# A fused attention and MoE kernel on one core: the first tokens' part with features on partitions, order-only edges behind it, 1 MB weight pieces

## The chip, the cores and the metric

One Trainium2 chip, of which the kernel uses one core. The metric is the device time of one execution in microseconds (us). The engines are named as in the profile: PE (TensorE matmul) and PEld (its weight loads), DVE (VectorE), ACT (ScalarE), POOL (GpSimd), SP (SyncE, which here issues every DMA).

## The reference

Attention with a local causal softmax and a linear memory, gated per head, then a squared-ReLU MLP over the tokens (B=4, H=8, S=576, D=64; 2304 tokens, d_model 512, d_ff 2048):

```python
scores = 1/sqrt(D) * q @ k.T                     # causal, softmax over keys
local = softmax(scores) @ v
q_p = where(q > 0, q, exp(q) - 1) + 1
mem_out = (q_p @ M_prev) / (q_p . z_prev + 1e-6)
g = sigmoid(beta)
x = g * mem_out + (1 - g) * local                # (B*S, 512)
out = relu(x @ w_in)**2 @ w_out
```

The weights come as 64-bit floats, so the kernel has to make numbers that TensorE takes from pairs of 32-bit words.

## The kernel before

Every matrix product of the MLP runs in three terms, high by high, high by low, low by high. `split_weight` makes the high and the low part of each weight piece (128 rows of 512 numbers, 32 pieces, 512 KB each): DVE shifts the low word (line 163), ACT scales the high word (164), DVE merges both (165), ACT copies the high part (168), DVE subtracts (169). Each piece comes by one DMA on SP's queue (line 193); pieces 0 to 11 are the first stage, 12 to 22 the second, 23 to 31 the third and fourth, and a later stage's raw buffers take the place of earlier ones.

The tokens are worked in blocks of 256. Block 0 is the first 64 tokens of each of the four sequences; their attention and memory part is `first_tokens` (two groups of two sequences). The MLP of block 0 (`moe(0)`) needs the result of `first_tokens` as `xh` and `xl`, then the weight pieces as they come. The other tokens' attention runs in units of one sequence, one pair of heads and two or four query tiles (`attention`), beside the MLP of earlier blocks. The last two blocks are done together by `moe_pair`, 512 columns at a time.

`first_tokens` before the change holds the query rows on partitions for the memory part: exp on ACT (272), two DVE operations to make phi (273, 274), a product with `z` and a sum over the features on DVE (275, 276), the norm (277 to 279) and a scaling (280). The softmax is: mask (285), maximum (288), subtract (289), exp over all 512 columns (290), sum (291), norm (292 to 294), scaling (295). `outputs` then transposes both halves with eight 128x128 matmuls per group (304), copies them by ACT (306), and multiplies with `v` and `M` in sixteen matmuls per group (315).

A scheduler sets the order of each engine's queue; `first_tokens` has high priority in it. The generators are merged as

```python
merge((attn(0, 1), 12), (wsteps(13), 12))
merge((attn(1, FIRST), 52), (wsteps(33), 20), (first(), 18))
```

so the first attention units, the weights and the first MLP block interleave. SP's transfers take eight semaphores in turn: each is issued only when the one eight places ahead of it has landed.

Of the kernel before, what the change touches and what calls it, by code (L numbers as in the profile page):

```python
# [12 lines left out]
U32 = mybir.dt.uint32  # L13
AF = mybir.ActivationFunctionType
# [7 lines left out]
P = 128  # L22
# [9 lines left out]
PAIR = 0  # L32
# [10 lines left out]
PXT = 'up'  # L43
# [12 lines left out]
SEQ = 'a0 b0 g a1 b1 c0 c1 r l r r r r'  # L56
# [9 lines left out]
TE = ['dd', 'dd', 'dd', 'dd', 'dd']  # L66
TC = 'aa'
TW = 2 * NP * 6 * D
GB = 2
GN = GB * NP  # L70
GD = GN * D
TAGS = [0, 16, 16, 16, 18]


FIRST = 4
AFTER = mybir.DependencyInfo(mybir.DependencyClass.NoSync, mybir.DependencyReason.DATA)
# [14 lines left out]
def fused_kernel(ctx: ExitStack, tc: tile.TileContext, t0_d, zt_d, kk_d, qv_d, beta, w_in, w_out, out):  # L91
# [14 lines left out]
    nc.vector.tensor_copy(identb, idt)  # L106
    mask = cp.tile([P, MW], BF16, name="mask")
# [13 lines left out]
    gpb = cp.tile([P, GN], F32, name="gpb")  # L121
    g1b = cp.tile([P, GN], F32, name="g1b")

    def gates():
        nc.scalar.activation(gpm, gpm, AF.Exp, scale=-1.0)
        nc.vector.tensor_scalar(out=gpm, in0=gpm, scalar1=1.0, scalar2=None, op0=ALU.add)
        nc.vector.reciprocal(gpm, gpm)
# [4 lines left out]

        for b in range(GB):
            nc.vector.tensor_copy(gpb[:, b * NP : (b + 1) * NP], gp)
        nc.vector.tensor_scalar(out=g1b, in0=gpb, scalar1=-1.0, scalar2=1.0, op0=ALU.mult, op1=ALU.add)
# [3 lines left out]
    nc.vector.tensor_copy(mask0[D:], mask[D:, 512 : 512 + D])  # L139

# [16 lines left out]
    def split_weight(n):  # L157
        for rw, c0, c1 in raw.pop(n):
# [4 lines left out]
            nc.vector.tensor_scalar(out=u0, in0=u0, scalar1=29, scalar2=None, op0=ALU.logical_shift_right)  # L163
            nc.scalar.activation(f1, f1, AF.Prelu, scale=2.0**-111, alpha=-(2.0**32))  # L164
# [60 lines left out]
    def first_tokens(tp, ahead):  # L225
        me, ze, se, xe, ye = ([nc.gpsimd if c == "p" else nc.vector for c in t] for t in TE)
# [5 lines left out]
        tr, sp, wt0, wx = ({} for _ in range(4))  # L232
# [3 lines left out]
        for step in SEQ.split():  # L236
            if step == "r":
                ahead()
            elif step == "l":
                nxt.append(loads(*order[0]))  # L240
            elif step == "g":
                load_beta()
            else:
                g = int(step[1])
                if step[0] == "a":
                    nc.sync.dma_start(tr[g][:, : 2 * GD], t0_d[g, :, : 2 * GD])
                elif step[0] == "b":
                    nc.sync.dma_start(tr[g][:, 2 * GD : 3 * GD], t0_d[g, :, 2 * GD : 3 * GD])
                    for h in range(2):
                        nc.sync.dma_start(  # L250
                            tr[g][h * D : (h + 1) * D, 3 * GD : 4 * GD], zt_d[2 * g + h].partition_broadcast(D)
                        )
                else:
                    nc.sync.dma_start(tr[g][:, 4 * GD :], t0_d[g, :, 3 * GD :])

        def part(g, o, n):
            return tr[g][:, GD * o : GD * (o + n)].rearrange("p (i x) -> p i x", i=GN)

        def scores(g):
            sp[g] = sp0[:, g]  # L260
            qd = tr[g][:, : 2 * GD].rearrange("p (r i d) -> p i r d", r=2, i=GN)
            for i in range(GN):
                for h in range(2):
                    hd = slice(h * D, (h + 1) * D)
                    nc.tensor.matmul(sp[g][hd, i], qd[hd, i, 0], qd[hd, i, 1], start=True, stop=True)

        def phi(g):
            qn, zb = part(g, 2, 1), part(g, 3, 1)
            wt0[g] = tp.tile([P, GN, P], F32, tag="w", name="w", bufs=2)
            f = wt0[g][:, :, D:]  # L270
            t2 = tp.tile([P, GN], F32, tag="t2", name="t2", bufs=2)
            nc.scalar.activation(f, qn, AF.Exp)
# [606 lines left out]
```

## Time and profile before

| what | us |
|---|---|
| three runs | 584.8, 581.32, 584.38 (median 584.38) |
| the profiled execution, its time | 583.52 |
| its span, first to last instruction | 581.7 |
| PE busy in the span | 544.9 |
| DVE busy | 406.3 |
| ACT busy | 349.3 |

Busy times are unions over an engine's instructions; neighbouring instructions of one engine overlap a little, so the distance from start to start is shorter than an instruction's own time. The execution's own time is 1.8 us more than its span. DMA moved 75.72 MB in all.

### The profile page before, as it was taken

The numbers are of one execution on the slowest core, as the hardware profiler recorded it, in microseconds if no ns is written. First come the engines' busy times: TensorE is split into PE (matmuls) and PEld (weight loads), VectorE is DVE, ScalarE is ACT, GpSimd is POOL, SyncE is SP. The second block draws the span as 40 slices with busy tenths as digits, with TensorE's granted clock in tenths as the row PEclk, the third lists the DMA queues.
The fourth block names the chain that finished last, engine by engine and source line by source line (L and its number), as shares of the span: only waits on it lengthen the run. The fifth ranks groups of instructions, "written<-read, shape, count | busy, mean of one in ns | idle before, by whom it ended". The sixth has DMA issues, their size and how long they took to land.

```text
span 581.7 us, 11097 instructions
## 1 busy us (share of the span) xinstructions
PE 544.9 (94%) x4019; PEld 469.7 (81%) x4019; DVE 406.3 (70%) x1338; ACT 349.3 (60%) x794; POOL 39.4 (7%) x36
## 2 busy tenths in 40 slices
PE   2179999999999999999999999999999999999996
PEld 2058888787889788888888889888889898888885
DVE  5999989979968788998796888869887422000000
ACT  2779897667867667797567665566756222222222
POOL 1100011010100000000000000000000000222221
PEclk9998999999999999999999999999999999999999
DMA  8959386666375458885554636585235400000001
GB/s 283 372 176 368 94 254 194 155 143 158 96 153 135 117 134 189 148 200 155 128 136 95 148 99 155 111 178 139 55 90 114 110 16 1 36 1 0 1 0 73
DMA packets 125462, 75.72 MB, mean 130 GB/s; under 512 B 97248, under 2 KB 110560, under 8 KB 125408
## 3 DMA queue, kind: packets, MB, share of 16 engines
q1 hardware_dynamic: 125408, 75.02, 48.8%
q8 instruction: 31, 0.51, 0.4%
q14 instruction: 23, 0.19, 0.1%
HBM read 42.63 MB, written 8.78 MB: 88 GB/s over the span
## 4 chain that ended last, share of the span: by engine, by line
PE 62%; DVE 22%; DMA 9%; ACT 4%; issue 2%; SPq 1%; ACTq 0%; DVEq 0%
PE oacc L713 6%; PE oacc L711 6%; PE oacc L712 6%; PE up L723 6%; PE up L722 6%; PE up L721 6%; PE sp L467 4%; DVE e L486 3%; PE up L672 2%; PE up L671 2%; PE up L670 2%; DVE a L546 2%; DMA aT<-a 2%; DVE w L169 2%; PE pm L435 2%
## 5 line engine op out<-in xcount | busy, mean ns | idle before, releaser
L721 PE MATMUL up<-xh,w 128*128 128x256 f32 x448 | 129.0, 288 | 0.9 <-ACT xh L319 0.7
L723 PE MATMUL up<-xh,w 128*128 128x256 f32 x448 | 129.3, 289 | 0.0
L722 PE MATMUL up<-xl,w 128*128 128x256 f32 x448 | 128.3, 286 | 0.3 <-DVE xl L320 0.3
L506 ACT ACTIVATE e<-e,mx 128x320 f32<-128x320 f32 (+3 forms) x128 | 77.7, 610 | 54.9 <-DVE memx L586 35.4
L721 PEld LDWEIGHTS up<-xh,w 128*128 128x128 f32 x448 | 86.3, 193 | 5.0 <-ACT xh L319 1.0
L711 PE MATMUL oacc<-w,gh 128*128 128x512 f32 x224 | 90.2, 403 | 0.0
L712 PE MATMUL oacc<-w,gh 128*128 128x512 f32 x224 | 88.9, 397 | 0.0
L722 PEld LDWEIGHTS up<-xl,w 128*128 128x128 f32 x448 | 86.2, 192 | 3.0 <-issue 0.6
L723 PEld LDWEIGHTS up<-xh,w 128*128 128x128 f32 x448 | 86.2, 192 | 1.3 <-issue 0.7
L713 PE MATMUL oacc<-w,gl 128*128 128x512 f32 x224 | 85.4, 398 | 0.8 <-DVE gl L733 0.8
L546 DVE SCALAR_TENSOR_TENSOR a<-e,a 128x128 f16<-128x128 f32 x116 | 66.0, 577 | 24.1 <-ACT a L544 23.6
L678 DVE CAST gh<-r 128x512 fp32r<-128x512 f32 x16 | 6.8, 428 | 78.6 <-ACT r L677 78.6
L544 ACT ACTIVATE a<-e 128x128 f16<-128x128 f32 x116 | 55.1, 525 | 9.5 <-DMA aT<-a 9.1
L727 ACT ACTIVATE r<-up 128x512 f32<-128x512 f32 x56 | 32.9, 588 | 42.6 <-PE up L723 25.2
L713 PEld LDWEIGHTS oacc<-w,gl 128*128 128x128 f32 x224 | 40.9, 188 | 9.3 <-DVE gl L733 1.9
L711 PEld LDWEIGHTS oacc<-w,gh 128*128 128x128 f32 x224 | 42.2, 188 | 7.5 <-ACT hw L164 0.8
L712 PEld LDWEIGHTS oacc<-w,gh 128*128 128x128 f32 x224 | 42.3, 189 | 6.6
L486 DVE CUSTOM_DVE_ANT_0 e<-sp,mask 128x320 f32<-128x320 f32 (+3 forms) x128 | 47.2, 415 | 0.0
L676 ACT ACTIVATE r<-up 128x512 f32<-128x512 f32 x16 | 9.6, 599 | 62.1 <-PE up L672 62.1
L679 POOL TENSOR_TENSOR gl<-r,gh 128x512 fp32r<-128x512 f32 x16 | 20.7, 1292 | 379.9 <-DVE gh L678 379.9
L733 DVE TENSOR_TENSOR gl<-r,gh 128x512 fp32r<-128x512 f32 x56 | 39.1, 699 | 2.9 <-ACT gh L730 1.7
L576 PE MATMUL acc<-vs,aT 128*128 128x128 f16 x302 | 36.5, 220 | 0.0
(153 smaller groups left out, 1131.1 us busy)
## 6 DMA issues: line engine op xcount, KB each, us to landing
raw<-in_w_in_dram SPq DMA_DIRECT2D x11, 512.0 KB, 8.3
vv<-in_qv_dram SPq DMA_DIRECT2D x16, 320.0 KB, 3.1
raw<-in_w_out_dram SPq DMA_DIRECT2D x9, 512.0 KB, 8.1
kd<-in_kk_dram SPq DMA_DIRECT2D x16, 288.0 KB, 3.2
out_dram<-o SPq DMA_DIRECT2D x16, 256.0 KB, 2.1
xd<-memx SPq DMA_DIRECT2D x31, 128.0 KB, 2.1
xn<-xd SPq DMA_DIRECT2D x14, 256.0 KB, 2.7
qm<-in_qv_dram SPq DMA_DIRECT2D x8, 321.0 KB, 3.1
```

The costliest lines, as they stand in the source:

```text
L486: nc.vector.tensor_tensor_reduce(out=e[:, h, ka:kb], in0=sps[:, h, cs], in1=mask[:, 448 - q0 + ka : 448 - q0 + kb], scale=-0.125, scalar=3 ...
L506: ex = nc.scalar.activation(e[:n, h, :ke], e[:n, h, :ke], AF.Exp, bias=bs, scale=-1.0, accum_out=sm[:n, h : h + 1])
L544: nc.scalar.mul(av[:, :, o0 : o0 + w], x, SC)
L546: nc.vector.scalar_tensor_tensor(out=av[:, :, o0 + w : o0 + 2 * w], in0=x, scalar=SC, in1=av[:, :, o0 : o0 + w], op0=ALU.mult, op1=ALU.sub ...
L576: nc.tensor.matmul(o2, aT[:, h * nb + c, :n], vs[:, h, c], start=False, stop=c == i)
L711: nc.tensor.matmul(acc[t], gh[:, u, ts], w_out_op(f, 0), start=f == 0, stop=False)
L712: nc.tensor.matmul(acc[t], gh[:, u, ts], w_out_op(f, 1), start=False, stop=False)
L713: nc.tensor.matmul(acc[t], gl[:, u, ts], w_out_op(f, 0), start=False, stop=f == NF - 1)
L721: nc.tensor.matmul(up[:, u, :], w_in_op(f, k, 0), xh[:, k, :], start=k == 0, stop=False)
L722: nc.tensor.matmul(up[:, u, :], w_in_op(f, k, 0), xl[:, k, :], start=False, stop=False)
L723: nc.tensor.matmul(up[:, u, :], w_in_op(f, k, 1), xh[:, k, :], start=False, stop=k == NK - 1)
L733: (nc.vector if n in GLV else nc.gpsimd).tensor_tensor(out=gl, in0=r, in1=gh.bitcast(F32), op=ALU.subtract)
```

## The change

- The first tokens' input comes as one array with features on partitions: `a` (q, k and z of a group, 128x1032) and `c` (M and v, 128x1024). The separate array of broadcast `z` rows is gone.
- The memory norm is made by TensorE: sixteen matmuls with one column (`nr`), a DVE operation and a reciprocal on 128x8, and sixteen matmuls that spread the result over the features (`rb`); DVE then scales phi by it. The softmax's subtraction and sum go into ACT's exp, which is issued eight times per group on 64 columns with a bias and an accumulator. Only the softmax is transposed (`px0`, sixteen 64x64 matmuls), and M and v are applied in 32 matmuls per group.
- Weight pieces in pairs (`PAIR = 1`): two pieces are one DMA of 1 MB and one instruction of 1024 columns per step, nine pairs in all. For pieces 0 to 7 the shift moves from DVE to ACT (an Identity over the top 16 bits).
- `later` adds edges that set order only: the weight shift of pieces from 8 and ACT's scaling of them, and the first attention unit's exp and matmuls, are queued behind the first tokens' operations of the same engine.
- The sequence of the first transfers changes (`SEQ`).
- `moe_pair`: the low part of the squared hidden values is made by DVE instead of POOL, the accumulators lie in other PSUM buffers, and the last matmuls are ordered so that one token tile after another ends and is written out.

```diff
-PAIR = 0
+PAIR = 1
-SEQ = 'a0 b0 g a1 b1 c0 c1 r l r r r r'
+SEQ = 'a0 g a1 r r c0 l r r c1'
+WE = 8
...
+    def later(eng, x):
+        if eng in gate:
+            tc.add_manual_dep(x.ins, gate[eng].ins.name, AFTER, reason="first tokens lead")
+        return x
...
-            nc.vector.tensor_scalar(out=u0, in0=u0, scalar1=29, scalar2=None, op0=ALU.logical_shift_right)
-            nc.scalar.activation(f1, f1, AF.Prelu, scale=2.0**-111, alpha=-(2.0**32))
+            if n < 8:
+                top = rw.bitcast(U16).rearrange("p n (t h) -> p n t h", h=2)[:, :, 0, 1]
+                nc.scalar.activation(u0, top, AF.Identity, scale=2.0**-13, bias=half[:, :1])
+            else:
+                later("v", nc.vector.tensor_scalar(out=u0, in0=u0, scalar1=29, scalar2=None, op0=ALU.logical_shift_right))
+            prelu = nc.scalar.activation(f1, f1, AF.Prelu, scale=2.0**-111, alpha=-(2.0**32))
+            if n >= WE:
+                later("s", prelu)
...
-            ze[g].tensor_tensor(out=zb, in0=zb, in1=f, op=ALU.mult)
-            nc.vector.reduce_sum(out=t2, in_=zb, axis=AX.X)
+            for i, hd in pairs():
+                nc.tensor.matmul(nr[hd, i : i + 1], f[hd, i], z[hd, i : i + 1], start=True, stop=True)
+            nc.vector.scalar_tensor_tensor(out=t2, in0=nr, scalar=1e-6, in1=gib, op0=ALU.add, op1=ALU.mult)
             nc.vector.reciprocal(t2, t2)
-            se[g].tensor_tensor(out=f, in0=f, in1=t2[:, :, None].to_broadcast(bc), op=ALU.mult)
+            for i, hd in pairs():
+                nc.tensor.matmul(
+                    rb[hd, i], t2[hd, i : i + 1].to_broadcast([D, D]), ident[hd, hd], start=True, stop=True
+                )
+            nc.vector.tensor_tensor(out=f, in0=f, in1=rb, op=ALU.mult)
...
-            xe[g].tensor_tensor(out=e, in0=e, in1=t1[:, :, None].to_broadcast(bc), op=ALU.subtract)
-            nc.scalar.activation(e, e, AF.Exp)
-            nc.vector.reduce_sum(out=t1, in_=e, axis=AX.X)
+            for i in range(GN):
+                nc.scalar.activation(
+                    e[:, i], e[:, i], AF.Exp, bias=t1[:, i : i + 1], scale=-1.0, accum_out=ts[:, i : i + 1]
+                )
...
-                for i in range(NP):
-                    nc.tensor.transpose(px[:, i], wt0[g][:, b * NP + i], ident)
+            for i, hd in pairs():
+                nc.tensor.matmul(px[hd, i], et[g][hd, i], ident[hd, hd], start=True, stop=True)
+            gate["s"] = nc.scalar.copy(ex, px)
...
+            for i, hd in pairs():
+                nc.tensor.matmul(xp[hd, i], m[hd, i], ft[g][hd, i], start=True, stop=False)
+                gate["t"] = nc.tensor.matmul(xp[hd, i], v[hd, i], ex[hd, i], start=False, stop=True)
...
-            nc.gpsimd.tensor_tensor(out=gl, in0=r, in1=gh.bitcast(F32), op=ALU.subtract)
+            nc.vector.tensor_tensor(out=gl, in0=r, in1=gh.bitcast(F32), op=ALU.subtract)
...
+        for x, tokens in ((three, (0, 1)), (two, (0, 1)), (one, (0, 1)), (two, (2,)), (one, (2,)), (two, (3,)), (one, (3,))):
+            mms = down(*x, tokens=tokens)
+            if x is one:
+                for t in tokens:
+                    evict(t)
```

How the queues stand. ACT's queue, first before, then after, from the exp of the second group's queries; `raw` are the weight words, `w` with a number a weight's high or low part, `w` alone the first tokens' softmax values, `t` its row maxima, and `e` the first attention unit's scores.

```order
L272 ACTIVATE w<-tr_119 128x8x64
L164 ACTIVATE raw_141<-raw_141 128x512
L380 ACTIVATE pe<-qm 128x256
L290 ACTIVATE w<-w 128x8x64 x2
L164 ACTIVATE raw_149<-raw_149 128x512
L168 CAST w_98<-raw_141 128x512
L164 ACTIVATE raw_151<-raw_151 128x512
L164 ACTIVATE raw_153<-raw_153 128x512
L506 ACTIVATE e,sm<-e,mx 128x320
```

```order
L282 ACTIVATE f<-tr_117 128x512
L178 ACTIVATE raw_133<-raw_133,half 128x1024
L181 ACTIVATE raw_133<-raw_133 128x1024
L178 ACTIVATE raw_135<-raw_135,half 128x1024
L181 ACTIVATE raw_135<-raw_135 128x1024
L187 CAST w_100<-raw_133 128x1024
L306 ACTIVATE w,ts<-w,t_267 128x64 x8
L306 ACTIVATE w,ts<-w,t_337 128x64 x3
L187 CAST w_101<-raw_135 128x1024
L306 ACTIVATE w,ts<-w,t_337 128x64 x4
L178 ACTIVATE raw_144<-raw_144,half 128x1024
L181 ACTIVATE raw_144<-raw_144 128x1024
```

Before, one weight piece stood ahead of the softmax's two exps; now two pairs stand ahead of sixteen, and two passes of the third pair ahead of the last one. The attention unit's exps are not in this stretch any more.

DVE's queue around the first tokens' softmax, first before, then after; `sp` are its scores, and `nr` is the new norm in PSUM.

```order
L285 SCALAR_TENSOR_TENSOR w<-sp_157,mask_86 128x8x64
L280 TENSOR_TENSOR w<-w,t_175 128x8x64
L288 TENSOR_REDUCE t_212<-w 128x8
L276 TENSOR_REDUCE t_202<-tr_119 128x8
L288 TENSOR_REDUCE t_254<-w 128x8
L163 TENSOR_SCALAR raw_141<-raw_141 128x512
L289 TENSOR_TENSOR w<-w,t_212 128x8x64
```

```order
L136 TENSOR_SCALAR gs<-gpm 128x8
L184 SCALAR_TENSOR_TENSOR raw_133<-raw_133 128x1024
L288 SCALAR_TENSOR_TENSOR t_167<-nr,gib 128x8
L300 SCALAR_TENSOR_TENSOR w<-sp_149,mask_88 128x512 x2
L289 RECIPROCAL t_167<-t_167 128x8
L303 TENSOR_REDUCE t_267<-w 128x8
L303 TENSOR_REDUCE t_337<-w 128x8
L184 SCALAR_TENSOR_TENSOR raw_135<-raw_135 128x1024
```

The merge of the first weight pair now stands ahead of the mask, and the sums and subtractions are gone.

PE's queue where the first MLP block begins, first before, then after; `up` is the MLP's first product, `acc` and `pxa` belong to the first attention unit, `pm` and `sp` to its memory part and scores.

```order
L521 MATMUL pxa<-identr,e 64x128
L521 MATMUL pxa<-identr,e 128x128
L721 MATMUL up<-xh,w_98 128x256
L565 MATMUL acc<-vv,aF 128x64 x6
L722 MATMUL up<-xl,w_98 128x256
L723 MATMUL up<-xh,w_98 128x256
```

```order
L323 MATMUL xp<-wx,tr_117 64x64
L481 MATMUL sp<-kd,qm 128x320 x2
L481 MATMUL sp<-kd,qm 128x192 x2
L447 MATMUL pm<-qm,pe 128x130 x2
L749 MATMUL up<-xh,w_100 128x256 x2
L750 MATMUL up<-xl,w_100 128x256
L751 MATMUL up<-xh,w_100 128x256
L749 MATMUL up<-xh,w_100 128x256
```

The last two of ten transposes `pxa` and six `acc` matmuls of the first attention unit are seen ahead of the MLP's products before; they and a second group of scores, further ahead, stand behind the MLP's first products now.

## Rows read from the trace of the kernel before

**Rows 1.** The page's first part: busy us, share of the span, instructions.

```profile
PE 544.9 (94%) x4019; PEld 469.7 (81%) x4019; DVE 406.3 (70%) x1338; ACT 349.3 (60%) x794; POOL 39.4 (7%) x36
```

**Rows 2.** Windows: length, busy us (instructions) of PE, PEld, DVE, ACT, POOL; clock, DMA share, GB/s.

```profile
0.00:5.00 5.00, 0.56 (x10) 0.56 (x12) 1.00 (x3) 1.58 (x2) 1.82 (x8) 1.00 0.64 198
5.00:10.00 5.00, 1.67 (x32) 1.48 (x30) 3.07 (x13) 0.84 (x2) 0.00 (x0) 1.00 0.99 283
10.00:15.00 5.00, 1.72 (x32) 1.53 (x30) 3.86 (x10) 0.63 (x1) 0.00 (x0) 1.00 1.03 383
20.00:25.00 5.00, 0.00 (x0) 0.00 (x0) 5.00 (x19) 3.82 (x11) 0.00 (x0) 1.00 1.04 412
45.00:50.00 5.00, 4.66 (x26) 4.45 (x26) 5.00 (x17) 5.00 (x15) 0.00 (x0) 0.66 1.03 417
50.00:100.00 50.00, 49.89 (x339) 42.14 (x337) 47.59 (x145) 44.10 (x110) 7.32 (x4) 1.00 0.63 203
100.00:150.00 50.00, 46.86 (x372) 39.31 (x373) 44.12 (x139) 36.03 (x78) 4.03 (x3) 1.00 0.62 146
150.00:577.00 427.00, 425.42 (x3107) 369.76 (x3105) 272.77 (x936) 236.73 (x537) 23.65 (x19) 1.00 0.42 100
```

**Rows 3.** Waits of PE from 0 to 60 us: total us, times, longest.

```profile
PE px L304 <- ACT w L168: 12.7, 1, 12.7
PE sp L265 <- DMA tr<-in_t_dram: 7.8, 2, 4.4
PE sp L467 <- DVE t L276: 4.4, 1, 4.4
```

**Rows 4.** Timeline of PE: start, length, what, wait before it and its releaser.

```profile
46.09 0.41 PE L722 MATMUL up<-xl,w 128*128 128x256 f32 x1 [0.34 <-DVE xl L320]
```

**Rows 5.** Timeline of SP and ACT: the first weight piece, two exps with accumulator.

```profile
6.73 0.64 SPq L193 DMA_DIRECT2D raw<-in_w_in_dram  x1
...
15.05 0.67 ACT L164 ACTIVATE raw<-raw 128x512 f32<-128x512 f32 x1 [3.94 <-DMA raw<-in_w_in_dram]
...
24.63 0.46 ACT L506 ACTIVATE e<-e,mx 128x192 f32<-128x192 f32 x1
...
25.08 0.45 ACT L506 ACTIVATE e<-e,mx 128x192 f32<-128x192 f32 x1
```

**Rows 6.** Timeline of DVE: two neighbouring operations of 512 columns.

```profile
13.50 0.68 DVE L285 SCALAR_TENSOR_TENSOR w<-sp,mask 128x512 f32<-128x512 f32 x1
14.10 0.68 DVE L280 TENSOR_TENSOR w<-w,t 128x512 f32<-128x512 f32 x1
```

**Rows 7.** Groups by form, DVE and ACT, 0 to 120 us: busy, mean ns of one.

```profile
L163 DVE TENSOR_SCALAR raw<-raw 128x512 uint32<-128x512 uint32 x20 | 8.3, 416 | 0.9 <-DMA raw<-in_w_in_dram 0.7 <-DMA raw<-in_w_out_dram 0.2
L546 DVE SCALAR_TENSOR_TENSOR a<-e,a 128x1024 f16<-128x1024 f32 x2 | 2.4, 1208 | 0.0
L544 ACT ACTIVATE a<-e 128x1024 f16<-128x1024 f32 x2 | 2.1, 1042 | 0.0
```

**Rows 8.** Timeline of PE: scores, attention output, transposes, scores at full clock.

```profile
32.78 2.08 PE L467 MATMUL sp<-kd,qm 64*128 64x320 f32 x8
...
43.78 1.97 PE L565 MATMUL acc<-vv,aF 64*128 64x64 f32 x12
...
52.35 0.82 PE L521 MATMUL pxa<-identr,e 128*64 128x128 f32 x6
53.10 1.13 PE L467 MATMUL sp<-kd,qm 64*128 64x320 f32 x8
```

**Rows 9.** Groups by form of PE, 35 to 46 us.

```profile
L315 PE MATMUL xp<-wx,tr 128*64 128x64 f32 x64 | 3.4, 260 | 0.0
```

**Rows 10.** Timelines of PE, ACT and SP at the end.

```profile
576.78 0.39 PE L665 MATMUL oacs<-w,gl 128*128 128x512 f32 x1
...
577.20 1.08 ACT L692 ACTIVATE o<-oacs 128x512 f32<-128x512 f32 x2
...
576.69 1.96 SPq L694 DMA_DIRECT2D out_dram<-o  x4
```

More of the change, by code (lines that the diff above doesn't have):

```diff
@@ L90, in fused_kernel @@
 @with_exitstack
[L91 removed]
+def fused_kernel(ctx: ExitStack, tc: tile.TileContext, t0_d, kk_d, qv_d, beta, w_in, w_out, out):
     nc = tc.nc
@@ L106, in fused_kernel @@
     nc.vector.tensor_copy(identb, idt)
+    half = cp.tile([P, 1], F32, name="half")
+    nc.vector.memset(half, 2.0**-14 - 0.5)
     mask = cp.tile([P, MW], BF16, name="mask")
@@ L231, in first_tokens @@
         bc = [P, GN, D]
-        tr, sp, wt0, wx = ({} for _ in range(4))
+        tr, sp, et, ft = ({} for _ in range(4))
         for g in range(ng):
@@ L256, in part, with pairs @@
-        def part(g, o, n):
-            return tr[g][:, GD * o : GD * (o + n)].rearrange("p (i x) -> p i x", i=GN)
+                c0, c1 = {"a": (0, TA), "q": (0, GD), "k": (GD, TA), "c": (TA, TW)}[step[0]]
+                nc.sync.dma_start(tr[g][:, c0:c1], t0_d[g, :, c0:c1])
+        def part(g, c):
+            return tr[g][:, c : c + GD].rearrange("p (i x) -> p i x", i=GN)
+        def pairs():
+            return [(i, slice(h * D, (h + 1) * D)) for i in range(GN) for h in range(2)]
         def scores(g):
@@ L260, in scores @@
             sp[g] = sp0[:, g]
[L261 to L265, printed above, removed]
+            q, k = part(g, 0), part(g, GD)
+            for i, hd in pairs():
+                nc.tensor.matmul(sp[g][hd, i], q[hd, i], k[hd, i], start=True, stop=True)
@@ L299, in outputs @@
-            vm = part(g, 4, 2)
-            for b in range(GB):
-                ws = slice(b * NP, (b + 1) * NP)
-                px = ps.tile([P, NP, P], F32, tag="up", name="px0", bufs=2)
-                for i in range(NP):
-                    nc.tensor.transpose(px[:, i], wt0[g][:, b * NP + i], ident)
-                if TC[g] == "a":
-                    nc.scalar.copy(wx[g][:, ws], px)
-                else:
-                    nc.vector.tensor_copy(wx[g][:, ws], px)
-            xp = ps.tile([P, GB, NP, D], F32, tag="av", name="xp", bufs=2)
@@ L310, in outputs @@
-            for b in range(GB):
-                for i in range(NP):
-                    n = b * NP + i
-                    for h in range(2):
-                        hd = slice(h * D, (h + 1) * D)
-                        nc.tensor.matmul(xp[hd, b, i], vm[:, n, hd], wx[g][:, n, hd], start=True, stop=True)
+            ex = tp.tile([P, GN, D], F32, tag="wx", name="wx", bufs=2)
+            px = ps.tile([P, GN, D], F32, tag="up", name="px0", bufs=2)
+            for i, hd in pairs():
+                nc.tensor.matmul(px[hd, i], et[g][hd, i], ident[hd, hd], start=True, stop=True)
@@ L379, in attention @@
         w = slice(qa, qb)
-        nc.scalar.activation(pe[:, w], q_raw[:, w], AF.Exp)
+        lead = (b, p, tiles) == order[0]
+        ex = nc.scalar.activation(pe[:, w], q_raw[:, w], AF.Exp)
+        if lead:
+            later("s", ex)
         ph = pe if sfull else q_raw
@@ L469, in scores @@
                             )
+                            if x == h == 0 and lead:
+                                later("t", mm)
                             if behind:
```

134 lines of the change are left out of this document (66 added, 68 removed).

## The prediction

> **What bounds the kernel now.** I read the page's busy shares first, then windows over the span, then PE's waits and the timelines at both ends. PE is busy 544.9 of 581.7 us, far more than any other engine [rows 1]. The windows show where it isn't: before 45 us it works little, from 50 to 100 us it lacks 0.11 us, from 100 to 150 us 3.14 us, and from 150 to 577 us 1.58 us [rows 2]. So the end is set by the moment from which PE runs without a break, plus its work from there. That moment is 46.09 us, when the low part `xl` of the first tokens' second group is there [rows 4]. Ahead of it PE's three long waits are for data (7.8 us), for DVE's sum over the features (4.4 us) and for the first tokens' scaled softmax ahead of the transposes (12.7 us; the view names the ACT copy that ended last) [rows 3]. DVE is busy all of 20 to 25 us [rows 2]. So a gain must come from an earlier dense start, and what PE did in the gaps before 46 us must not be forgotten: work that leaves the gaps comes back behind the dense start.
>
> **The first tokens, when PE's dense start comes.** The walk goes along ACT's queue after the change, which has most to do.
> Landing of the weights: before, the first piece was the last of 3.68 MB queued (inputs of the first tokens 3.15 MB, the piece 0.52) and ACT began on it at 15.05 us [rows 5]. By 15 us 0.99 + 1.42 + 1.92 = 4.32 MB had moved [rows 2], so a piece is there when some 0.64 MB behind it has moved too. Now the second pair ends at 3.16 MB of the queue (two `a` of 0.53, beta, two pairs of 1.05). With 0.64 MB that is 3.80 MB; 0.99 MB at 5 us and 383 to 412 GB/s from there [rows 2] give 12.2 us.
> From there ACT has eight passes of 1024 columns (scaling and Identity of the second to fourth pair, two copies) and sixteen exps ahead of its copy of `px0`. A pass of 1024 columns is 1.04 us [rows 7], with overlap 1.0. An exp with accumulator on 192 columns takes 25.08 - 24.63 = 0.45 us from start to start [rows 5]; at 0.7 ns a column by the rows of 1024 and 192 columns (1042 against 460 ns), 64 columns are 0.36, sixteen 5.8. So 12.2 + 8.0 + 5.8 = 26.0 us, and 26.6 with the copy of 512 columns (0.6, estimated from the same rows).
> Then PE's 32 matmuls of group 0. The 32 of both groups before were 64 instructions in 3.4 us of busy time [rows 9], so 32 per group take 3.4: 30.0 us. ACT's `xh` and the second copy follow, 1.2: 31.2, and PE's group 1: 34.6. PE then has the scores (2.08 [rows 8]) and `pm` (0.7, estimated from the same row by eight against four instructions, less): 37.4. DVE, from the first `xh` at 30.6, has five 512-wide operations at 0.60 [rows 6], two more subtractions and `xl` at about 0.6 each and eight of 256 columns or a shift at about 0.34 (half of 512): some 7 us and 0.5 of waiting on ACT, 38.1. PE's dense start is then 38.1, **8.0 us earlier**. The ends of this price: 36.5 if a pair lands without the 0.64 MB lag, 45.3 if transfers share evenly (rival below).
>
> A page that speaks against the split of the exps and against my price at once: the Trainium skill, ScalarE: Activation LUTs, section What ACT_TABLE_LOAD costs, puts an ACTIVATE with a pointer bias at 280 ns + 0.833 ns a column and the overlap of neighbours at 93 ns. By that sixteen exps of 64 columns would be an estimated 3.8 us without the accumulator reads that stand in the trace, and the sum below 2.0 us lower. The measured spacing decides, so I keep 5.8; against two exps of 512 columns either is a loss on ACT, which the other removals on its queue don't cover.
>
> **What comes back behind the dense start.** Before, eight score instructions, ten transposes and twelve output instructions of the first attention unit were done ahead of 46.09; now they stand behind the MLP's first products. At PE's dense pace: 1.13 us for eight scores, 10 x 0.82/6 = 1.4 for the transposes, 1.97 for the twelve [rows 8]: **+4.5 us**. The one low-clock stretch stays: the granted clock averages 0.66 of the full 2.4 GHz from 45 to 50 us, thus 1.2 GHz part of the time [rows 2], and I let it cost the same behind the new start.
>
> **DVE and ACT behind it.** DVE loses per group a product, a sum, a subtraction and another sum, 4 x 0.60 [rows 6], and four operations on 128x8; twice that is 5.4 us. Eight shifts of 0.42 [rows 7] go to ACT, 3 us; eighteen wide operations save one overhead each, 2 x 0.60 against 1.21 less overlap, 0.07 us or 1.3 us. With 0.5 of additions DVE is some 9 us lighter. ACT gets four Identity passes (4.0) and sixteen exps for two (+4.6), loses two copies (1.2) and overheads (1.3): some 6 us heavier, with 5.9 us free from 50 to 100 us and 14 free from 100 to 150 [rows 2]. The bounds of this exchange: PE's waits after the dense start were 4.8 us (0.11 + 3.14 + 1.58). DVE's slack can take up to the 3.1 from 100 to 150 us; in-order queues with wide pieces can add as much: before PE's first down-product ACT has the pairs' passes and DVE four pairs to do, where I count 1.9 us of waiting by the same walk, and 0.8 at the second. I take old and new waits as equal, **0**, between -3.1 and +3.4.
>
> **The other edits.** `later` removes no work; it is the cause of the 4.5 us above, and its cover is that PE is dense there in either case. The wide DMAs move the same bytes. SP's queue is moved past the first tokens' `c` and the units' loads: 1 MB buffers of the second stage wait for DVE's subtraction of the third and fourth pair, at some 29 us, and land by 36, when DVE needs them at 39; if they were 3 us later, the cost would be that difference. In `moe_pair` DVE has room (272.77 busy of 427 [rows 2]), so its `gl` costs nothing. At the end PE's last matmul starts at 576.78, ACT evicts two tiles behind it in 1.08 us, and SP issues the last of four transfers at the end of 576.69 + 1.96 [rows 10]. Now one tile stays behind: half of 1.08, **-0.5 us**, with ends of 0 and -1.0.
>
> **The sum.** -8.0 + 4.5 + 0 - 0.5 = -4.0 from the profiled 583.52: **579.5 us**. That execution is 0.9 below the median of the runs shown (584.38), so the same gain from the median would be 580.4.
>
> **Rivals.**
> *The weights come late (slower).* On DVE the merge of the first pair, on ACT both pairs, stand ahead of the softmax. If the outstanding transfers share the bandwidth evenly, the second pair is whole only with all that was issued by then: 6.9 MB by about 19.4 us at the same rates, 7.2 us later. Dense start 45.3, end 586.7. It decides from a landing at 16.2 us (12.2 + 4.0). For it: a piece issued at 6.73 was used at 15.05 [rows 5]. Against: that lag was 0.64 MB, not everything. The Trainium skill, DMA: Bandwidth & Descriptors, section Queues, rings and completion order, states that "completion is **not FIFO per issuing engine**"; no run here shows how far. By that rule alone the end would be the 586.7 above. If `c` of the second group, needed by PE's first matmul of group 1 ahead of the last transposes, is caught too, the loss passes 1%.
> *The gain is eaten (no change).* PE is ready earlier than ACT and DVE can serve the MLP: the waits grow by the full 3.4 us: 582.9. For it: ACT's added 6 us, both engines busy over 44 of 50 us from 50 to 100 [rows 2]. Against: DVE is 9 us lighter, and the weights come earlier.
> *All of it goes well (faster).* The waits from 100 to 150 us go (-3.1) and the clock does not drop at the dense start (the 1.7 us that 0.34 of five us cost): 574.7. For it: DVE is the lighter one of the two in that stretch. Against: PE has only small matmuls ahead of its dense start.
>
> **How the numbers follow.** The forecast, 577 to 582.5, has 0.52; weights late 0.15; gain eaten 0.18; all well 0.15. About 1% (5.8 us) is what a measurement of this kernel can tell from no change. Of the forecast 0.25 lies past it, with all of the last case: faster 0.40. Half of the late case, where the second wait adds to the first, is slower by over 1%: 0.08. The rest, 0.52, is within 1%. The range runs from 573.5 (the best case with an earlier landing) to 587.0 (the late case); the forecast's own range is 577 to 582.5.
>
> **What would show it.** Right: PE's first wait-free MLP product near 38 us and PE dense from there; ACT's sixteen exps near 5.8 us; the attention unit's transposes behind it; DVE busy some 9 us less, but for the 16 subtractions taken from POOL; one ACT eviction behind PE's last matmul. Wrong: the first merge of a pair on DVE later than 14 us, the dense start past 41, or new PE waits for `gh` and `gl` over 4 us in all.

## The result, and the profile after

| | before | after |
|---|---|---|
| median of four runs each, us | 583.9 | 589.66 |
| ratio, 95% interval | | 1.0106 (1.0077 to 1.0134) |
| profiled execution, its time / its span, us | 583.52 / 581.7 | 589.49 / 587.7 |
| start of PE's dense work | 46.09 | 38.60 |
| PE's last matmul ends | 577.17 | 583.99 |

By the ratio the change is 1.06% slower. The forecast was 579.5, with 587.0 as the upper end of the range.

The first 40 us went as worked out. The timelines of ACT, DVE and PE after the change show the second pair's first pass at 12.15 (forecast 12.2), the first merge on DVE at 11.91, the first exp, the start of the copy of `px0` at 25.98 (26.0), and PE's first product with `xl`, behind which it lacks only 0.7 us up to 100 us, at 38.60 (38.1):

```profile
12.15 1.28 ACT L178 ACTIVATE raw<-raw,half 128x1024 uint32<-128x1024 uint16 x1 [0.27 <-DMA raw<-in_w_in_dram]
...
11.91 1.23 DVE L184 SCALAR_TENSOR_TENSOR raw<-raw 128x1024 uint32<-128x1024 uint32 x1 [2.45 <-ACT raw L181]
...
15.31 0.35 ACT L306 ACTIVATE w<-w,t 128x64 f32<-128x64 f32 x1
...
15.65 0.34 ACT L306 ACTIVATE w<-w,t 128x64 f32<-128x64 f32 x1
...
25.98 0.56 ACT L318 COPY wx<-px 128x512 f32<-128x512 f32 x1
...
38.60 0.39 PE L750 MATMUL up<-xl,w 128*128 128x256 f32 x1 [0.79 <-DVE xl L329]
```

Two exps stand 0.34 us apart from start to start (I had 0.36). The last line answers to [rows 4]: 7.5 us of the forecast 8.0 are there.

The windows after, which answer to [rows 2] (length, then busy us and instructions of PE, PEld, DVE, ACT, POOL, then clock, DMA share, GB/s):

```profile
50.00:100.00 50.00, 49.75 (x310) 42.16 (x310) 40.68 (x118) 41.68 (x107) 3.54 (x3) 1.00 0.42 137
100.00:105.00 5.00, 2.76 (x26) 1.49 (x24) 3.84 (x21) 1.04 (x2) 0.00 (x0) 1.00 0.87 161
105.00:110.00 5.00, 2.34 (x13) 1.75 (x15) 4.27 (x10) 2.47 (x7) 0.84 (x1) 0.80 1.01 258
110.00:115.00 5.00, 5.00 (x24) 4.13 (x22) 4.72 (x22) 2.35 (x4) 0.00 (x0) 0.51 0.79 99
108.04:114.86 6.82, 5.67 (x25) 4.54 (x25) 6.16 (x24) 4.27 (x9) 0.80 (x1) 0.50 0.91 138
115.00:150.00 35.00, 32.53 (x285) 27.06 (x285) 29.16 (x93) 26.17 (x57) 4.04 (x3) 1.00 0.69 154
150.00:450.00 300.00, 296.23 (x2420) 260.48 (x2419) 249.05 (x874) 205.63 (x480) 3.47 (x4) 1.00 0.61 133
450.00:584.00 134.00, 134.00 (x721) 114.30 (x719) 39.21 (x95) 39.05 (x69) 0.00 (x0) 1.00 0.11 28
38.60:583.99 545.39, 533.52 (x3861) 461.69 (x3861) 382.24 (x1254) 328.09 (x743) 12.85 (x11) 0.99 0.48 114
```

The kernel before, in the stretches that [rows 2] joins, and from its dense start to PE's last matmul, as the last line above has it:

```profile
150.00:450.00 300.00, 298.42 (x2453) 262.18 (x2452) 252.60 (x890) 204.49 (x481) 2.97 (x3) 1.00 0.57 133
450.00:577.00 127.00, 127.00 (x655) 107.58 (x653) 20.17 (x47) 32.24 (x57) 20.68 (x16) 1.00 0.07 21
46.09:577.17 531.08, 526.24 (x3832) 455.12 (x3832) 368.39 (x1229) 320.92 (x735) 34.99 (x26) 1.00 0.47 116
```

From 100 to 110 us PE is busy 5.10 of 10 us. From 108.04 to 114.86 us the granted clock is 1.2 GHz (0.50 of the full clock), also behind 110 us, where PE has no gap any more. From 50 us to PE's last matmul it lacks 4.8 us before (527.17 less 522.3 busy) and 11.4 after (533.99 less 522.6); from its dense start 4.8 (531.08 less 526.24) and 11.9 (545.39 less 533.52). DVE's relief is there too, 91.7 us busy from 50 to 150 before [rows 2] and 82.7 after, yet it shows as idle time.

What PE waits for, from 100 to 150 us after:

```profile
PE acc L587 <- DMA aT<-a: 1.8, 1, 1.8
PE acc L587 <- DVE memx L458: 1.6, 1, 1.6
PE sp L481 <- DMA kd<-in_kk_dram: 1.1, 1, 1.1
PE pm L447 <- DVE s L594: 0.9, 1, 0.9
PE px L637 <- DMA xn<-xd: 0.9, 1, 0.9
PE sp L481 <- DVE mx L502: 0.7, 1, 0.7
PE oacc L741 <- DVE gl L761: 0.2, 1, 0.2
```

All but the last belong to the attention units or to the transposes `px` that turn their results into MLP block 1's input. The place is seen in PE's timeline: block 0's seven first steps are done at 100, and its eighth (L749) starts only at 111.62, at half the clock:

```profile
99.95 0.61 PE L447 MATMUL pm<-qm,pe 128*128 128x130 f32 x4
...
102.36 0.23 PE L587 MATMUL acc<-vs,aT 128*128 128x128 f16 x1 [1.81 <-DMA aT<-a]
...
105.56 0.95 PE L637 MATMUL px<-identr,xn 128*128 128x128 f32 x6 [0.85 <-DMA xn<-xd]
...
107.55 0.81 PE L447 MATMUL pm<-qm,pe 128*128 128x130 f32 x4 [0.90 <-DVE s L594]
109.50 2.18 PE L481 MATMUL sp<-kd,qm 64*128 64x448 f32 x8 [1.15 <-DMA kd<-in_kk_dram]
111.62 0.58 PE L749 MATMUL up<-xh,w 128*128 128x256 f32 x1
...
113.91 0.41 PE L750 MATMUL up<-xl,w 128*128 128x256 f32 x1
...
116.00 0.28 PE L751 MATMUL up<-xh,w 128*128 128x256 f32 x1
```

Before, the same place had down products of block 0 (L711 to L713) left to cover the units' latency:

```profile
103.40 0.44 PE L621 MATMUL px<-identr,xn 128*128 128x128 f32 x3
103.67 0.46 PE L711 MATMUL oacc<-w,gh 128*128 128x512 f32 x1
...
105.58 0.73 PE L713 MATMUL oacc<-w,gl 128*128 128x512 f32 x2 [0.75 <-DVE gl L733]
...
110.48 0.38 PE L721 MATMUL up<-xh,w 128*128 128x256 f32 x1
```

So the transposes start 2.2 us later than before (105.56 against 103.40), and the eighth step 1.1 us later (111.62 against 110.48), though the dense work began 7.5 us earlier. The units are late: the second unit's keys are asked for at 39.60 after and at 22.12 before, and the transfer of results (`xd`) that is third in the run goes out at 100.29 against 84.03. SP's timeline, first before (its first row joins two loads, at 22.12 and 34.90), then after:

```profile
22.12 13.11 SPq L337 DMA_DIRECT2D kd<-in_kk_dram  x2
...
84.03 0.54 SPq L597 DMA_DIRECT2D xd<-memx  x1
```

```profile
39.60 0.38 SPq L346 DMA_DIRECT2D kd<-in_kk_dram  x1
...
81.84 0.92 SPq L350 DMA_DIRECT2D qm<-in_qv_dram  x2
97.28 0.33 SPq L353 DMA_DIRECT2D vv<-in_qv_dram  x1
97.72 2.04 SPq L566 DMA_TRANSPOSE aT<-a  x1
100.29 0.40 SPq L613 DMA_DIRECT2D xd<-memx  x1
```

One link of the lateness is seen here: a load of values stands from 82.8 to 97.28, when the third unit's products have ended and give its buffer back, with the fourth unit's transposing DMA behind it. SP's waits have the 14.5 us under `vt`, PE's matmul behind those products.

```profile
SPq L353 <- PE vt L416: 14.5, 1, 14.5
```

The chain of work that ended last, followed back from the last instruction, says where the units' products stood before that. In the changed kernel it runs from 52.0 to 96.9 us through PE alone, whose matmuls each follow the one ahead in the queue, then through DVE, ACT, the transposing DMA and the next load of keys to the eighth step. In the kernel before, some 34 of the 47 us from 50 to 97 are DVE's, more than half of it work on the weights. So from 52 us on the units' products waited for their turn among block 0's in PE's order. That this order makes the loss isn't shown by the chain. Four pieces of it after the change (start, length, what):

```profile
94.82 0.98 PE acc L581 x5
95.80 1.12 PE sp L481 x5
...
100.80 2.88 DMA aT<-a
...
105.32 4.05 DMA kd<-in_kk_dram
```

At the end one eviction stands behind PE's last matmul instead of two [rows 10]:

```profile
583.15 0.84 PE L679 MATMUL oacc<-w,gz 128*128 128x512 f32 x3
...
584.03 0.60 ACT L687 ACTIVATE o<-oacc 128x512 f32<-128x512 f32 x1 [0.76 <-PE oacc L679]
...
581.72 3.27 SPq L688 DMA_DIRECT2D out_dram<-o  x4
```

### The profile page after: what moved, and what is told of

Its sections match the earlier page's. It is cut to its first block, busy times and chain, and to the rows that moved or that the text cites. A ratio compares the mean times of both kernels' runs of the same rounds, so it can differ in the third digit from the quotient of the medians.

```text
span 587.7 us, 11537 instructions
## 1 busy us (share of the span) xinstructions
PE 555.9 (95%) x4259; PEld 482.4 (82%) x4259; DVE 409.3 (70%) x1314; ACT 357.7 (61%) x808; POOL 15.5 (3%) x20
## 4 chain that ended last, share of the span: by engine, by line
PE 59%; DVE 15%; DMA 11%; ACT 9%; issue 3%; SPq 2%; ACTq 0%; DVEq 0%
PE oacc L679 7%; DMA aT<-a 6%; PE oacc L739 6%; PE oacc L740 5%; PE oacc L741 5%; PE up L749 5%; PE up L751 5%; PE up L750 5%; PE sp L481 4%; DVE a L562 3%; DVE e L502 3%; PE up L695 2%; PE up L694 2%; PE up L693 2%; ACT a L560 2%
## 5 line engine op out<-in xcount | busy, mean ns | idle before, releaser
L749 PE MATMUL up<-xh,w 128*128 128x256 f32 x448 | 130.2, 291 | 2.4 <-ACT xh L328 1.9
L750 PE MATMUL up<-xl,w 128*128 128x256 f32 x448 | 130.1, 290 | 0.8 <-DVE xl L329 0.8
L749 PEld LDWEIGHTS up<-xh,w 128*128 128x128 f32 x448 | 86.7, 194 | 5.3 <-ACT xh L328 2.1
L739 PE MATMUL oacc<-w,gh 128*128 128x512 f32 x224 | 89.9, 401 | 0.3 <-ACT gh L758 0.3
L562 DVE SCALAR_TENSOR_TENSOR a<-e,a 128x128 f16<-128x128 f32 x116 | 64.4, 569 | 36.6 <-ACT a L560 35.6
L740 PE MATMUL oacc<-w,gh 128*128 128x512 f32 x224 | 88.4, 394 | 0.0
L679 PE MATMUL oacc<-w,gh 128*128 128x512 f32 x120 | 36.8, 389 | 0.0
```

The source lines that it names most:

```text
L562: nc.vector.scalar_tensor_tensor(out=av[:, :, o0 + w : o0 + 2 * w], in0=x, scalar=SC, in1=av[:, :, o0 : o0 + w], op0=ALU.mult, op1=ALU.sub ...
L679: mms.append(nc.tensor.matmul(acc[t], g[:, ts], w_out_op(f, part), start=s0, stop=s1))
L739: nc.tensor.matmul(acc[t], gh[:, u, ts], w_out_op(f, 0), start=f == 0, stop=False)
L740: nc.tensor.matmul(acc[t], gh[:, u, ts], w_out_op(f, 1), start=False, stop=False)
L749: nc.tensor.matmul(up[:, u, :], w_in_op(f, k, 0), xh[:, k, :], start=k == 0, stop=False)
L750: nc.tensor.matmul(up[:, u, :], w_in_op(f, k, 0), xl[:, k, :], start=False, stop=False)
```

## The experiments

Ratios are against the kernel before on the same chip; the changed kernel's is 1.0106. "Lack" is the time from 50 us to PE's last matmul less PE's busy time in it, of one profiled execution. The changed kernel lacks 11.4, the kernel before 4.8.

**Parts of the change undone.** Three theories: A, the units are late and block 1 waits for them; B, ScalarE's added load; C, the wide pieces.

```diff
 e1: -        lead = (b, p, tiles) == order[0]
     +        lead = False
 e2: -        if eng in gate:
     +        if False and eng in gate:
 e3: -            if n < 8:
     +            if n < 0:
 e4: -PAIR = 1
     +PAIR = 0
```

> The changed kernel without its three order-only edges on the first attention unit (its exp, its first memory product and its score batches no longer stand behind the first tokens); the edges on the weights stay. Theory A, the boundary: block 1 of the MLP starts when the first four attention units have delivered its input, in the changed kernel at 111.6 us although block 0 is done by 100, and these units come late since their first one stands behind the first tokens and their small products stand behind block 0 in TensorE's order. Then the units end earlier without the edges, block 1 starts at 105 to 109, the second stretch at the lower clock (108 to 115) goes, and the time is 582 to 586 us, though the dense start may be up to 3 us later. Theory B, ScalarE's added load (some 6 us of exps, copies and bit moves) holds the units back: the load stays, 588 to 591. Theory C, the wide weight pieces block the queues: they stay, 588 to 591.

Measured: 599.21, ratio 1.026 (1.0192 to 1.0328). The first unit's scores went back to 15.9 us, but the third unit's came at 58.9 and block 0's first product at 43.7 (37.31 in the changed kernel); the eighth step started at 118.1. Lack 16.8.

> The changed kernel without any of the order-only edges behind the first tokens (weights and first unit). Theory A: as without the unit's edges, block 1 starts by 109 us and the time is 582 to 587, with a dense start later than 38.6, by up to 5 us, since the weight pieces take turns with the first tokens again: a later dense start and a shorter time together would say that the dense start is not what sets the end. Theories B and C: the load and the pieces stay, so the loss around 100 us stays and the dense start comes later on top: 590 to 595.

Measured: 601.24, 1.0291 (1.0254 to 1.0329). First product 45.5, eighth step 116.7, lack 12.8. The first product came later as expected, and the time did not fall but rose.

> The changed kernel with the top bits of the first eight weights moved by VectorE's shift again, as before, instead of ScalarE's Identity: about 8 x 1.2 us go from ScalarE to VectorE over the first 90 us. Theory A: VectorE stood idle for 45 percent of 85 to 100 us, so the units are not held back by either engine's load but by TensorE's order and the loads behind it; 588 to 592. Theory B (ScalarE's added load): the units end earlier, 583 to 586. Theory C: no change, 588 to 591.

Measured: 600.6, 1.0278 (1.0239 to 1.0316); dense start 39.2 (38.6), lack 19.0. The units did not end earlier, as B had it: the second unit's scores came at 58.3 us (54.0 in the changed kernel), with ScalarE's load taken back. That speaks against B and doesn't exclude it, since VectorE carries the load then.

> The changed kernel with the first stage's weights in pieces of 512 columns again (the PAIR constant 0), all else as changed. Theory A: the boundary stays, 588 to 592 (the first pieces may land earlier or later by a microsecond). Theory C (a wide piece holds VectorE, ScalarE and the load queue for twice as long, so that the units' short steps wait behind it): the loss around 100 us goes, 583 to 586. Theory B: 588 to 591.

Measured: 596.55, 1.0213 (1.0175 to 1.025); lack 13.7. From 100 to 150 us 8.2 us are missing, 7.4 in the changed kernel: the loss there is the same without wide pieces, and C is out as its cause.

All three theories missed: whichever of the four is taken out, the loss grows.

**The units served sooner, or their wait covered.** No work is changed in these six.

```diff
 e5: -KB = 1
     +KB = 2
 e6: -VVB = 2
     +VVB = 3
 e8: -            elif j == PJ and n + 1 < NBLK:
     +            elif j == (PJ if n else NF // 2 - 1) and n + 1 < NBLK:
 e7, e17, e18: the first matmul of block 0's step j, up (Uj) or down (Dj), behind
 the last matmul of the k-th finished token tile of the units, counted from 0
     +        k = HOLD.get(step)
     +        if n == 0 and k is not None and k < len(tiles_out):
     +            tc.add_manual_dep(mm.ins, tiles_out[k].ins.name, AFTER, reason="units lead")
 e7:  HOLD = {'U3': 1, 'U4': 3, 'U5': 4, 'U6': 5, 'D4': 5, 'D5': 6}
 e17: HOLD = {'D5': 6, 'D6': 7}
 e18: HOLD = {'U4': 2, 'U5': 4, 'U6': 5, 'D5': 6}
```

> The changed kernel with two buffers instead of one for the unit's keys (KB = 2). Theory D, the late units: the first unit's scores stand behind the first tokens (33.7 us against 16.1 before), they hold the one key buffer, so the second unit's keys are asked for at 39.6 instead of 22.1 and each of the first four units is 10 to 20 us later; block 1's transposes wait for the fourth, and they stand in TensorE's order and in the ring of the up accumulators ahead of block 0's eighth step. With two buffers the second unit's keys are there in the first 20 us, its scores follow the first's before 45 us, block 0's eighth step starts at 104 to 109 instead of 111.6, and the time falls to 580 to 586 us. Theory E, only the schedule's scatter (any edit throws the order of the whole program, and the place of 100 us is no worse than others): anything from 588 to 600, without a link to the time of the second scores.

Measured: 592.51, 1.0149 (1.0098 to 1.0199). The second unit's scores came at 43.2 instead of 54.0 as wanted, and the gain was gone by the third (60.9 against 62.8): the eighth step started at 110.7. Lack 14.3. A miss for D.

> The changed kernel with three buffers instead of two for the values (VVB = 3). At 82.8 us a load of values stands in the load queue until the third unit's last product gives its buffer back (14.5 us, to 97.3), and the fourth unit's transposes by DMA stand behind it (97.7), though what they read is done by 91. Theory D2: this block in the queue is the last link; with a third buffer the transposes start by 93, block 0's eighth step starts at 105 to 108, and the time is 582 to 587. Theory D with the units late for other reasons (TensorE's order): the transposes come earlier by up to 2 us only, 587 to 591.

Measured: 595.9, 1.02 (1.0147 to 1.0253). The fourth unit's products came 1.0 us earlier (101.3 against 102.4), the eighth step at 114.9. With the buffer there the transposing DMA still went out only at 96.9 us (97.7). The block in SP's queue is not the last link.

> The changed kernel with order-only edges that put steps of block 0 behind the units on TensorE: the up products of steps 4 to 7 behind the second, fourth, fifth and sixth finished token tile of the units, the down products of steps 5 and 6 behind the fifth and seventh. Theory D, in the form that block 0 stands in the units' way in TensorE's order while it has time: the units end earlier, block 0's last products cover their latency, the waits between 100 and 112 us go, block 0's eighth step starts at 103 to 108 and the time is 581 to 586. If the units are held by the other engines or by their loads, TensorE waits for them earlier instead, at the edges: 588 to 594.

Measured: 591.41, 1.0131 (1.007 to 1.0191). This is the clearest of the six. Its windows:

```profile
80.00:100.00 20.00, 17.86 (x116) 15.64 (x115) 14.74 (x54) 13.15 (x37) 0.84 (x1) 0.91 0.40 111
100.00:112.00 12.00, 12.00 (x81) 8.74 (x80) 8.54 (x21) 6.45 (x13) 0.85 (x1) 1.00 0.56 141
112.00:150.00 38.00, 33.38 (x282) 28.34 (x281) 30.74 (x108) 27.14 (x59) 3.74 (x3) 0.96 0.68 150
150.00:450.00 300.00, 294.73 (x2433) 259.49 (x2432) 256.18 (x904) 207.79 (x485) 2.81 (x3) 1.00 0.62 134
```

The waits from 100 to 112 us are gone altogether, and the eighth step starts at 110.0, earlier than in the kernel before (110.5). In their place 2.1 us are missing ahead of it, 4.6 from 112 to 150 and 5.3 up to 450: lack 12.3 against 11.4. The waits moved.

> The changed kernel with block 1's transposes behind block 0's eighth step instead of its seventh (for block 0 alone), so that the eighth step's 24 products (some 2.9 us) and its down products need not wait for the units. Theory D: 3 to 5 us of the waits at 100 to 112 us are covered, 584 to 588. If the waits only move behind the eighth step, where block 1 has to wait for the same units: 588 to 591.

Measured: 597.83, 1.0239 (1.0186 to 1.0293); lack 16.0, of it 10.6 from 150 to 450 us. The eighth step went ahead at 94.4, and the waits moved to the places behind it, with interest.

> The changed kernel with two order-only edges: block 0's sixth and seventh down steps stand behind the seventh and eighth finished token tile of the units, so that 24 products (some 5.5 us) are left to cover the units' last waits at 100 to 112 us, as in the kernel before. If the boundary's waits are the loss: they fall by 4 us, the second low-clock stretch goes, 582 to 587. If waits only move on, as with the edges that put more of block 0 behind the units: 588 to 594.

Measured: 590.22, 1.0114 (1.0064 to 1.0165); its profiled execution took 587.73, less than the median. The first `px` no longer waits for its transfer (0.9 us in the changed kernel), but a later one waits 1.2 us for `memx`, and the waits for scores grew from 1.8 us to 3.0:

```profile
PE sp L481 <- DVE mx L502: 3.0, 2, 1.9
PE px L640 <- DVE memx L602: 1.2, 1, 1.2
```

```profile
110.00:125.00 15.00, 13.09 (x100) 10.72 (x100) 12.17 (x44) 9.65 (x21) 1.43 (x1) 0.77 0.59 136
```

The first fence has PE's two longest waits from 100 to 130 us, the second the window 110 to 125: the low clock came all the same (0.77). Lack 9.2.

> The changed kernel with order-only edges on block 0's up steps 5 to 7 behind the third, fifth and sixth finished token tile and its sixth down step behind the seventh: a weaker form of the units' lead, without the waits at 80 to 90 us that the stronger form had. If the boundary's waits are the loss: 582 to 587; if they move on: 588 to 594.

Measured: 592.05, 1.0147 (1.0093 to 1.0202); lack 14.3, 8.8 of it from 150 to 450 us. They moved again. Lack by stretch, us:

| kernel | 50 to 100 | 100 to 150 | 150 to 450 | 50 to PE's end |
|---|---|---|---|---|
| before | 0.1 | 3.1 | 1.6 | 4.8 |
| changed | 0.2 | 7.4 | 3.8 | 11.4 |
| e7 | 2.4 | 4.6 | 5.3 | 12.3 |
| e17 | 2.2 | 3.3 | 3.7 | 9.2 |
| e18 | 1.7 | 3.6 | 8.8 | 14.3 |

All three shorten the waits at 100 to 150 us, and none of the ratios falls.

**Parts of the change alone, on the kernel before.**

```diff
 e10: moe_pair of the changed kernel in the kernel before
 e11: first_tokens, its input and first transfers (SEQ) of the changed kernel, and the PSUM
      tag of pxa (PXT, 'up' before, 'av' now), without edges, pairs, Identity and the new moe_pair
 e12: -PAIR = 0
      +PAIR = 1
 e13: the three edges on the first unit (lead) in the kernel before
 e14: e10, and the Identity of the changed kernel for pieces 0 to 7
 e15: e10, and the Identity for pieces 8 to 15
```

> The kernel before with the changed moe_pair alone: subtractions of the last stage on VectorE instead of GpSimd, the second half of the accumulators in another tag, and each token tile finished and sent before the next. By my sum the tail is worth 0.5 us (0 to 1.0): 583 to 584.5, as long as the order ahead of it stays. By theory E it may be off by several microseconds if the order ahead of it changes.

Measured: 581.74 against 583.7, 0.9976 (0.9952 to 1.0001). Behind PE's last matmul (579.35) stand 3.75 us of the span of 583.1, against 4.5 before; the profiled execution took 584.93, more than the median. It is the one kernel of the study that is not behind the kernel before; its interval reaches 1.

> The kernel before with the new computation of the first tokens alone: no order-only edges, narrow pieces, all bit moves on VectorE, the old last stage. My sum gave the early dense start to the whole; without the edges the first attention unit and the weights take their turns again, so a dense start between 41 and 46 us. Theory D: the units lead block 0 again as before (first scores by 17 us), no loss at the boundary, 580 to 585. Theory E: scatter, 587 to 600, with the loss in waits of TensorE spread over the run.

Measured: 593.77, 1.0192 (1.015 to 1.0233). Block 0's first product is at 47.6 us (43.5 before), and PE's dense start, the first product with `xl`, at 52.0 (46.1): later than before, where 41 to 46 was expected. The first two units' scores came early, at 14.6 and 28.5, and the third unit's at 62.1 (53.1 before). The new part makes PE wait at more places, among them for the norm's reciprocal (4.7 us) and for `xl` (4.2), and what stands behind in its queue waits too. Lack 8.1. A miss for D.

> The kernel before with the first stage's weights in pieces of 1024 columns (PAIR 1) and nothing else. Theory C, wide pieces cost by holding the in-order engines and the queue: 588 to 592, with a later dense start than 46.1. Theory D: no loss beyond a later dense start, 583 to 588. Theory E: scatter, anything up to 596.

Measured: 587.68, 1.0082 (1.0056 to 1.0109); dense start 47.2, lack 8.0. Alone the wide pieces come out slower; in the changed kernel it is slower without them (e4).

> The kernel before with the changed kernel's three order-only edges on the first attention unit alone (exp, memory product and score batches behind the first tokens); the first tokens themselves, the pieces and the tail stay as before. Theory D, late units cost the time wherever they come from: the first unit's scores go from 16 to 33 us or later, the third transfer of unit results (84 us before) comes at 95 or later as in every kernel with the new first tokens (97 to 104), the last load of block inputs at 470 or later, and the time is 588 to 600. If late units cost nothing: within 3 us of the kernel before.

Measured: 588.36, 1.0102 (1.0073 to 1.0132). The scores went to 35.6 and the last load of block inputs to 470, but the third transfer only to 88, and the dense start slipped to 52.7 as well. With a lack of only 3.6 the loss is the dense start's here, and the clock's (0.93 on average from 50 to 100 us, 1.00 before), so this does not settle what late units cost.

> The kernel before with two parts of the change that leave its units early: the bit moves of the first eight weights on ScalarE instead of VectorE, and the new last stage. Before, VectorE is busy 104.4 of the 110 us from 10 to 120 and the chain of waits there is VectorE's bit work, so theory D expects the units to gain: third transfer by 82, last load of block inputs by 462, 576 to 582. Theory E: the reordering decides, 580 to 590.

Measured: 589.21, 1.0111 (1.0065 to 1.0158); lack 11.9.

> As the kernel before with the new last stage and the bit moves on ScalarE, but those of the second eight weights instead of the first eight, whose split falls into the units' first stretch (50 to 110 us) and not into the first tokens'. Theory D: the units gain there, the first tokens stay: 577 to 582. Theory E: 580 to 590.

Measured: 591.85, 1.0159 (1.0129 to 1.0189); lack 11.3. The edit of e14 goes with a gain in the changed kernel (e3 takes it back and loses 1.7 points of ratio) and with a loss of some 1.4 here (e14 against e10). The load moved is the same; the order is not.

**Order alone.** No instruction is added, removed or changed.

```diff
 e9:  -    merge((attn(1, FIRST), 52), (wsteps(33), 20), (first(), 18))
      +    merge((attn(1, FIRST), 52), (wsteps(33), 20), (first(), 22))
 e16: -FIRST = 4
      +FIRST = 5
```

> The kernel before, with no instruction added, removed or changed: only the weight with which block 0's steps are merged with the units and the weights goes from 18 to 22, which lets the scheduler put them in another order from the second step of block 0 on (146 rows of ScalarE's and 282 of VectorE's stand elsewhere). Theory E, the order of the whole program is what a change of any kind throws, by several microseconds, and the kernel before had a good one: 587 to 596. Theory D (the changed kernel's loss is due to its late units alone): within 2 us of the kernel before, 582 to 586.

Measured: 587.04, 1.0075 (1.0043 to 1.0106). Its lack is 9.7 against 4.8, with 6.3 in the stretch

```profile
150.00:450.00 300.00, 293.69 (x2398) 258.29 (x2397) 245.16 (x865) 199.49 (x472) 1.77 (x2) 0.99 0.56 131
```

> The changed kernel with no instruction added, removed or changed: five units instead of four (FIRST) are merged with block 0, which lets the scheduler order the program otherwise from about 100 us on. Theory E, in the form that any other order of the same work lies some microseconds off and the published ones are picked: 591 to 600. Theory D: what counts is when the units' results and the last block inputs come; the time follows the last load of block inputs by about 117 us (the 112.7 behind it to the last product, and the tail), wherever that falls.

Measured: 596.14, 1.0218 (1.0165 to 1.027), against 1.0106 for the changed kernel in its own order; lack 18.9. The dense start is as in the changed kernel (37.12 for the first product, 37.31 there).

## Why the prediction was wrong

- **The dense start: right, with some luck on the way.** 8.0 us forecast, 7.5 measured. The weights were not late, and the first rival fell: by 12.1 us 3.68 MB had moved, 0.52 MB more than the queue up to the second pair, where 0.64 was forecast. But the rate behind the 12.2 us had no ground: [rows 2] have 283 GB/s from 5 to 10 us, and with them the pair would have been due at 13.6; that it was 380 after the change was not worked out. On ACT the eight passes took 0.5 us more than forecast and the sixteen exps 0.4 less. PE was through with `pm` at 35.4 instead of 37.4, which was worth nothing, since DVE's queue came last, as said. The terms given for that queue add up to 7.5 us, not to "some 7", and so to a start at 38.6; the trace has 38.60.
- **The work that comes back: right.** From its dense start to its last matmul PE is busy 526.24 us before and 533.52 after, +7.3. The stretch at 1.2 GHz behind 100 us cost half of the 5.67 us that PE was busy in it, 2.8, and the one at the dense start is in both sums; what is left is 4.5, as forecast.
- **The tail: right.** -0.8 (4.5 to 3.7 us behind PE's last matmul), forecast -0.5 with an end of -1.0; e10 has the same.
- **"I take old and new waits as equal, 0": this step failed.** From the dense start on they went from 4.8 to 11.9 us, +7.0, twice the upper end of 3.4. I had bounded them by the waits for `gh` and `gl` at the first down products, and those were harmless (0.5 us in all up to 150 us). The waits came from the attention units. I had deferred the first unit's matmuls and counted their PE time, and not that a chain of transfer, scores, exps, transposes and output hangs on each, that the next unit's keys wait for the same buffer, and that block 1's `px` stands in PE's order ahead of block 0's eighth step. "The gain is eaten" had the right mechanism in general, waits of PE for engines not ready in time, and allowed for half of their growth.
- **"The one low-clock stretch stays": incomplete.** It did stay (0.68 of the full clock from 40 to 45 us), and one more (0.66 from 25 to 30 us) lay ahead of the dense start, where the sum doesn't count it. But another followed the waits at 100 us: +2.8.
- **"What would show it: wrong"** named a late merge, a late dense start and waits for `gh` and `gl`. None of the three came. The list looked where I had done the sum.

Together: -7.5 + 4.5 + 7.0 + 2.8 - 0.8 = 6.0, and the profiled executions differ by 5.97.

What is shown and what isn't. Shown: where the time is, waits of PE for the units and the low clock behind them (profile); that the time doesn't hang on the first place of these waits alone, since three ways of covering it (e7, e17, e18) cut the lack from 100 to 150 us to between 3.3 and 4.6 and left the ratio at 1.011 to 1.015, e7 without a single gap from 100 to 112; and that the order of one and the same work is worth about as much as this whole change, +0.75% in the kernel before (e9), about +1.1% in the changed one (e16). Not shown: what each part of the change costs or gains by itself. Three of them came out slower alone (e11, e12, e13) and the changed kernel came out slower without each of four (e1 to e4), by 0.8 to 1.9 points of ratio. That would be so if the parts count on each other; it would also be so if both kernels stand in orders that happen to be good, since each of these edits puts the program in another order too, and two runs of order alone don't tell how wide that spread is. No run separates the two. One part, which the list of the change doesn't name, was never tried alone: `pxa` moved from the PSUM tag of the MLP's products to that of the units' (PXT). Open: what one cause throws the waits into the later stages, and whether there is an order in which the changed kernel keeps its 3.8 us of less work (7.5 - 4.5 + 0.8). The tries at one here did not find it. That late units cost by themselves is argued from the profile; e13 didn't isolate it.

## What to carry to other kernels

When a block of dense work is started earlier, follow its end as well: the time is gained only if what comes behind it is ready earlier too, so walk the second chain (here four attention units, through loads, buffers and queues) to the point where the dense work runs out. Work that is put behind an order-only edge moves with its whole chain and with every buffer that it holds, not with its PE time alone. And where a scheduler sets the order of a packed program, measure some orders of unchanged work first: what they differ by (0.75 and 1.1% for the two tried here) belongs in the range of any forecast, and a part taken out says little as long as its effect isn't larger.

## What was unexpected of the hardware

The granted clock fell to 1.2 GHz from 108.04 to 114.86 us, in the middle of the program, where PE was busy 5.10 of the 10 us from 100 to 110, and stayed there into dense work: a matmul of 256 columns took 0.41 us at 113.91 and 0.28 at 116.00. The kernel before shows no such stretch after 50 us. An Identity that reads 16-bit words and writes 32-bit ones over 1024 columns took 1.24 us, more than the scaling of as many columns (1.15); I had both at 1.04.
